# Where the triangular product of the routing gets its counts, and which PSUM banks some small products use

## The chip, the cores and the metric

The kernel runs on one core of one Trainium2 chip. The metric is the device time of one execution in microseconds (us). Engines are called PE or TensorE (matrix products), DVE or VectorE, ACT or ScalarE, POOL or GpSimd, and SP or SyncE (which here only issues transfers). A PSUM bank is 128 x 512 words of fp32 into which TensorE's products go and from which VectorE and ScalarE read them.

## What is computed

Three steps on 4 x 3584 = 14336 tokens of D = 192: a causal depthwise convolution of 7 taps, then a mixture of 8 experts (F = 1024), of which each token takes the best one, unless a skip gate lets the token pass, then a second mixture of 8 experts whose gate has a bias by modality. Cut to what matters:

```python
# convolution: 8 heads of 24 channels, softmax over the 7 taps of each head
out = np.einsum('hk,bskhg->bshg', w, x_unf)
# first mixture
do_compute = x @ w_skip > 0
xc = x[do_compute]
logits = xc @ w_gate
e_idx = np.argmax(logits, axis=1)
gate_w = softmax(logits)[e_idx]
y[e_idx == e] = gate_w * (np.maximum(xc @ w1[e], 0) @ w2[e])
out[do_compute] = xc + y
# second mixture: every token, no residual
logits = x @ w_gate2 + modality_bias[modality_id]
out[e_idx == e] = gate_w * (np.maximum(x @ w1[e], 0) @ w2[e])
```

The routing in between is done on the chip: every token of an expert gets a rank among that expert's tokens, and from the ranks come the lists by which the tokens are gathered in slots of 128.

## The kernel before, in words

**Stages.** The first stage runs over 128 tiles of 112 tokens, in NG = 8 groups of GT = 16 tiles, and each group has eight steps. A step (`run` of the first class, one value of `v`) does, for three groups that are at different points: six transposes of two tiles (`tr`, into bank 6 or 2), the rest of the preceding convolution product and the sum of the gate's halves on VectorE (`lows`, tiles `hl` and `L`), one head's convolution product (`conv`, banks 5, 0, 1 in turn), and the gate products of the tiles that were transposed two steps ago (`gm`, banks 7 and 4). Once per group `fin` makes gates and expert codes out of `L`, mostly on GpSimd, and SyncE stores the group's rows. After 64 + 12 steps the stage is over. When the lists of the first four groups (GA = 4) are there, the expert products begin (`Ffn`, slots of 128 tokens: gather, transposing transfer `xt`, products with `w1b` and `w2b`); the remaining steps of the first stage are done ahead of the first slots. In the last twelve steps the transposes use banks 6 and 5, and the gate products bank 7 and the words 352 to 487 of bank 5, since bank 2 belongs to the experts by then.

**Side work.** Beside these steps run generator tasks. Each `tick()` moves every task on by one; a task that did `yield n` sleeps for n ticks. A step has two ticks, at its `lows` and at its end. The routing of a group is such a task, `route_a`: it compares the codes with the eight expert numbers (`oha`), runs VectorE's scan over the 128 flags of each partition (`cuma`, 8 experts by 16 tiles, one running count), takes from the scan's last column of each expert the running totals `genda`, subtracts neighbours to get the counts `cnta`, multiplies these with a triangular matrix and one of ones (`tri`, `ones`: how many tokens lie on partitions below, and how many in all), copies the result from PSUM (`offa`), corrects the running counts on GpSimd, reduces them to `rank`, and turns ranks into slots and places (`sla`, `qa`), from which comparisons (`oa`, `ob`) and 16 products make the list. Two marks hand over between groups: a group starts when `res["A"]` has its number, and goes on to `rank` when `res["B"]` has it. The later routes (`ranks` and `invert`, called by `route`) do the same for more tokens with all of it on VectorE; they run while the experts run. Another set of tasks prepares the weights (scaled and split, tiles `w1b`, `w2b`, `ws`), with small products in banks 7 and 3.

**What sets the order.** Every engine works off its instructions as the program issues them: a wrapper (`InOrder`) ties each instruction to the one issued before it on its engine. So an instruction that waits holds up everything behind it, and where a task is after how many ticks decides what stands ahead and behind.

**Names.** Lines 126 to 139 hand out the banks: `misca` is 16 words of bank 3 for the product of `route_a`, `misc` 16 words of bank 3 for other small results and the product of `ranks`, `gram` the results of the preparation of weights (bank 7), `ptr1` and `pgt1` the transposes and gate products of the last twelve steps (lines 136 to 138), `acc` the lists (banks 3 and 5). Lines 401 to 414 hold the counts, the product and the correction, lines 440 and 441 the mark `res["A"]`, lines 481 to 504 `ranks`.

Nearly all instructions go through the wrapper and stand at line 70 in the profile, so they are told apart by the names of their tiles.

Of the kernel before, what the change touches and what calls it, by code (L numbers as in the profile page):

```python
# [7 lines left out]
F32 = mybir.dt.float32  # L8
# [4 lines left out]
ALU = mybir.AluOpType  # L13
# [14 lines left out]
GT = 16  # L28
# [86 lines left out]
class Moe:  # L115
    def __init__(self, tc, ctx):
# [4 lines left out]
        bk = [bp.tile([128, 512], F32, name=f"bank{i}") for i in range(8)]  # L121
        h = [b.bitcast(F16) for b in bk]
# [3 lines left out]
        self.acc = [bk[3], bk[5]]  # L126
        self.pt, self.pt2 = [h[4][:, 0:384]], [h[7][:, 512:896], h[3][:, 0:384]]
        self.pg2 = [bk[5][:, i:i + 64] for i in (0, 64, 128)]
        self.gram = [bk[7][:, 256:512], bk[7][:, 0:256]]
        self.misc = bk[3][:, 496:512]  # L130
        self.ph3 = bk[5]
        self.misca = bk[3][:, 240:256]
        self.pc0 = [bk[i][:TP, :384] for i in (5, 0, 1)]
        self.ptr0, self.ptr1 = ([h[i][:, :6 * TP] for i in p] for p in ((6, 2), (6, 5)))
        self.pgt0, self.pgt1 = ([bk[i][:, 0:136] for i in p] for p in ((7, 4), (7,)))
        self.pgt1.append(bk[5][:, 352:488])
        self.gramx = bk[3][:, 384:512]
# [236 lines left out]
    def route_a(self, g, code, pool, ob, res):  # L374
        nc = self.nc
# [5 lines left out]
        base = res["base"]  # L381
# [10 lines left out]
        oh = pool.tile([128, 8, GT], F32, name="oha")  # L392
        nc.vector.tensor_tensor(oh, cg.unsqueeze(1).to_broadcast([128, 8, GT]), self.c8.unsqueeze(2).to_broadcast([128, 8, GT]), ALU.is_equal)
        cum = pool.tile([128, 8, GT], F32, name="cuma")
# [3 lines left out]
        gend = pool.tile([128, 9], F32, name="genda")  # L398
        nc.gpsimd.memset(gend[:, 0:1], 0.0)
        nc.gpsimd.tensor_copy(gend[:, 1:9], cum[:, :, GT - 1])  # L400
        cnt = pool.tile([128, 8], F32, name="cnta")
        nc.gpsimd.tensor_tensor(cnt, gend[:, 1:9], gend[:, 0:8], ALU.subtract)
        pos = pool.tile([128, GT], F32, name="posa")
        nc.gpsimd.tensor_scalar(pos, cg, -float(SB * 128), float(8 * SB * 128), ALU.mult, ALU.add)
        yield 3
        pp = self.misca
        nc.tensor.matmul(pp[:, 0:8], self.tri, cnt, start=True, stop=True)
        nc.tensor.matmul(pp[:, 8:16], self.ones, cnt, start=True, stop=True)
        yield 2
        off = pool.tile([128, 16], F32, name="offa")  # L410
        nc.vector.tensor_copy(off, pp)
        nc.gpsimd.tensor_tensor(gend[:, 0:8], base, gend[:, 0:8], ALU.subtract)
        nc.gpsimd.tensor_tensor(gend[:, 0:8], gend[:, 0:8], off[:, 0:8], ALU.add)
        nc.gpsimd.tensor_tensor(base, base, off[:, 8:16], ALU.add)
        if g == GA - 1:
# [22 lines left out]
        nc.gpsimd.tensor_tensor(ok[:, 0], ok[:, 0], cg, ALU.mult)  # L438
        nc.gpsimd.tensor_tensor(cg, cg, ok[:, 0], ALU.subtract)
        yield 5  # L440
        res["A"] = g + 1
        for h in (2 * g, 2 * g + 1):
# [37 lines left out]

    def ranks(self, code, pool, lag, r, wait=4):
        nc = self.nc
# [9 lines left out]
        nc.vector.tensor_copy(gend[:, 1:9], cum[:, :, T - 1])  # L492
        cnt = pool.tile([128, 8], F32, name="cnt")
        nc.vector.tensor_tensor(cnt, gend[:, 1:9], gend[:, 0:8], ALU.subtract)
        yield wait
        pp = self.misc
        nc.tensor.matmul(pp[:, 0:8], self.tri, cnt, start=True, stop=True)
        nc.tensor.matmul(pp[:, 8:16], self.ones, cnt, start=True, stop=True)
        yield 2
        off = pool.tile([128, 17], F32, name="off")  # L500
        nc.vector.tensor_copy(off[:, 0:16], pp[:, 0:16])
        nc.vector.tensor_tensor(off[:, 0:8], off[:, 0:8], gend[:, 0:8], ALU.subtract)
        r.extend((oh, cum, off[:, 0:8], off[:, 8:16]))
        yield 1
# [869 lines left out]
```

## Time and profile before

| | before |
|---|---|
| median of 3 runs | 1078.73 us (1071.69 to 1083.71) |
| the profiled execution's own time | 1078.92 us, span 1077.1 us |
| granted clock of TensorE, mean | 0.941 |
| TensorE, matrix products busy | 967.9 us, 90% of the span |
| TensorE, weight loads (beside the products) | 802.2 us, 74% |
| VectorE busy | 688.7 us, 64% |
| ScalarE busy | 501.1 us, 47% |
| GpSimd busy | 628.5 us, 58% |
| moved by DMA | 165.35 MB |

Busy shares are averages over the whole span. The page cuts the span in 40 slices (27 us each): TensorE is busy for 6 to 8 tenths in the first 240 us and for 9 tenths or more in nearly all of the last two thirds. A matrix product counts as busy for as long as it takes, and takes twice as long where the clock is granted at 0.50; a clock of 1.00 is the full one. In a timeline a row may stand for several like instructions (x2, x16), and the brackets at its end say how long the engine stood idle before it and whose end it waited for.

### The profile page before, as it was taken

Reading aid. Unit: us, or ns where it says so; the run is one execution under the profiler, and the core shown is the slowest. Engines: PE = TensorE matmul, PEld = TensorE weight load, DVE = VectorE, ACT = ScalarE, POOL = GpSimd, SP = SyncE. Lnnn points to the kernel's source line nnn. Section 1 sums busy time; section 2 is a strip of 40 time slices with the busy share of each in tenths; the row PEclk is TensorE's granted clock in tenths of the full one; section 3 lists DMA queues with packets and bytes.
Section 4 is the critical chain, followed back from the end, with each engine's and each line's share of the span. In section 5 each row is a group of like instructions: output and inputs, shape, how many; then the busy total and the mean of one; then the engine's idle time right before and its main releaser. Section 6 shows DMA issues by size and latency. Waiting matters only on the chain. (4 is left out here: it accounts for less than half of the span.)

```text
span 1077.1 us, 27331 instructions
## 1 busy us (share of the span) xinstructions
PE 967.9 (90%) x10104; PEld 802.2 (74%) x10104; DVE 688.7 (64%) x1797; ACT 501.1 (47%) x919; POOL 628.5 (58%) x1113
## 2 busy tenths in 40 slices
PE   6688877799999879999899999999999899999993
PEld 4556666688888767888777877778787788888882
DVE  4376966769998889888446666667844344444441
ACT  3485743443665535455345555553233333333331
POOL 4044778776856836676447877774443555545531
PEclk9887876999999889999999999999999999999997
DMA  5666457665669737767973443333257333323340
GB/s 203 210 205 246 153 169 217 172 199 160 208 181 267 229 121 244 221 204 219 292 229 98 95 110 101 96 101 91 53 151 242 78 73 75 76 72 72 79 117 14
DMA packets 109135, 165.35 MB, mean 154 GB/s; under 512 B 80976, under 2 KB 86074, under 8 KB 103233
## 3 DMA queue, kind: packets, MB, share of 16 engines
q1 hardware_dynamic: 94368, 134.02, 39.9%
q0 software_dynamic: 13920, 28.87, 11.9%
q8 instruction: 81, 1.33, 0.5%
q10 hardware_dynamic: 704, 0.63, 0.2%
q14 instruction: 62, 0.50, 0.2%
HBM read 181.56 MB, written 58.42 MB: 223 GB/s over the span
## 5 line engine op out<-in xcount | busy, mean ns | idle before, releaser
L70 PEld LDWEIGHTS <-w1b 128*128 128x128 f16 x4840 | 374.4, 100 | 54.1 <-issue 18.5
L70 PE MATMUL bank<-xp,w1b 128*128 128x256 f16 x2200 | 263.7, 273 | 8.2 <-DMA w1b<-s1b 2.5
L70 PEld LDWEIGHTS <-ws 128*128 128x128 f16 (+2 forms) x2208 | 192.1, 100 | 67.0 <-DMA ws<-in_moe_w_dram 10.9
L70 PE MATMUL bank<-w2b,ws 128*128 128x384 f16 x1760 | 237.4, 286 | 0.2 <-issue 0.2
L70 DVE SCALAR_TENSOR_TENSOR ws<-bank,ws 128x512 f16<-128x512 f32 x220 | 151.4, 690 | 124.3 <-ACT ws L70 105.6
L70 POOL DMA_INDIRECT out_dram<-u,si x114 | 115.4, 1013 | 185.2 <-DVE u L70 58.7
L70 ACT ACTIVATE ws<-bank 128x512 f16<-128x512 f32 x220 | 130.6, 597 | 113.5 <-PE bank L70 102.7
L70 PE MATMUL bank<-xt,w1b 128*128 128x128 f16 x2640 | 170.1, 225 | 10.7 <-DVE hlo L70 6.9
L70 PE MATMUL bank<-w2b,hh 128*128 128x384 f16 x528 | 141.2, 334 | 1.0 <-DMA w2b<-s2a 1.0
L70 PE MATMUL bank<-w2b,hlo 128*128 128x192 f16 x528 | 131.8, 250 | 0.0
L70 ACT ACTIVATE u<-bank,c 128x192 f32<-128x192 f32 x114 | 48.1, 422 | 153.2 <-PE bank L70 118.1
L70 DVE SCALAR_TENSOR_TENSOR hlo<-bank,hh 128x512 f16<-128x512 f32 x132 | 90.3, 686 | 42.2 <-ACT hh L70 41.3
L70 DVE SCALAR_TENSOR_TENSOR u<-bank,c,u 128x192 f32<-128x192 f32 x114 | 47.6, 417 | 100.5 <-ACT u L70 84.5
L70 ACT ACTIVATE hh<-bank 128x512 f16<-128x512 f32 x132 | 76.7, 593 | 42.1 <-PE bank L70 40.7
L70 PEld LDWEIGHTS <-hh 128*128 128x128 f16 x528 | 53.4, 101 | 31.5 <-issue 3.3
L70 POOL DMA_INDIRECT gt<-rows,idx x64 | 64.0, 999 | 11.2 <-issue 9.3
L70 PE MATMUL bank<-xg,band 128*112 128x384 f32 x128 | 64.0, 593 | 0.3 <-DVE s L70 0.3
L70 ACT COPY xtb<-bank 128x672 f16<-128x672 f16 x64 | 46.5, 728 | 36.9 <-PE bank L70 36.5
L70 POOL DMA_INDIRECT gt<-rows,idxB x56 | 56.5, 1008 | 11.9 <-issue 7.0
L70 POOL TENSOR_TENSOR x2s<-x2s,xs 128x192 f32<-128x192 f32 x46 | 31.6, 688 | 53.7 <-DVE x2s L70 42.2
L70 PE MATMUL bank<-ob,oa 128*128 128x56 f16 (+2 forms) x446 | 49.7, 263 | 6.0 <-DVE ob L70 6.0
L70 PEld LDWEIGHTS <-hlo 128*128 128x128 f16 x528 | 52.9, 100 | 1.6 <-issue 1.5
(252 smaller groups left out, 1431.8 us busy)
## 6 DMA issues: line engine op xcount, KB each, us to landing
w1b<-s1b SPq DMA_DIRECT2D x59, 1024.0 KB
w2b<-s2b SPq DMA_DIRECT2D x59, 768.5 KB
ws<-in_moe_w_dram SPq DMA_DIRECT2D x16, 768.0 KB
rows<-hl SPq DMA_DIRECT2D x8, 1386.0 KB
xg<-in_x_dram SPq DMA_DIRECT2D x7, 1536.0 KB
ws<-in_moe_w_dram SPq DMA_DIRECT2D x16, 512.0 KB
ws<-in_moe_w_dram SPq DMA_DIRECT2D x32, 256.0 KB
s1a<-w1b SPq DMA_DIRECT2D x8, 1024.0 KB
```

The costliest lines, as they stand in the source:

```text
L70: r = f(*args, **kw)
```

## The change

In `route_a` the subtraction of neighbours moves behind the product. Instead of the counts the two products multiply the scan's last column of each expert (`cum[:, :, GT - 1]`, eight words 16 apart), and the differences are taken from the product's result. For that, `offa` has two rows of nine words with a zero ahead of each, and `cnta` is now the 2 x 8 differences, on GpSimd. The product is issued one tick later after the scan (4 for 3), the copy of its result one tick later after the product (3 for 2). `res["A"]` is set five ticks earlier, so the next group may start while this one still compares. In `ranks` the same is done on VectorE, and the wait ahead of the product goes from 4 to 6 ticks. Then banks: `misc` and the second `gram` go from banks 3 and 7 to bank 4, the gate products of the last twelve steps from bank 5 to bank 4; a list `pt` that nothing used goes.

```diff
-        self.pt, self.pt2 = [h[4][:, 0:384]], [h[7][:, 512:896], h[3][:, 0:384]]
+        self.pt2 = [h[7][:, 512:896], h[3][:, 0:384]]
         self.pg2 = [bk[5][:, i:i + 64] for i in (0, 64, 128)]
-        self.gram = [bk[7][:, 256:512], bk[7][:, 0:256]]
-        self.misc = bk[3][:, 496:512]
+        self.gram = [bk[7][:, 256:512], bk[4][:, 0:256]]
+        self.misc = bk[4][:, 496:512]
         self.ph3 = bk[5]
         self.misca = bk[3][:, 240:256]
         self.pc0 = [bk[i][:TP, :384] for i in (5, 0, 1)]
         self.ptr0, self.ptr1 = ([h[i][:, :6 * TP] for i in p] for p in ((6, 2), (6, 5)))
-        self.pgt0, self.pgt1 = ([bk[i][:, 0:136] for i in p] for p in ((7, 4), (7,)))
-        self.pgt1.append(bk[5][:, 352:488])
+        self.pgt0, self.pgt1 = ([bk[i][:, 0:136] for i in p] for p in ((7, 4), (7, 4)))
@@ route_a
         nc.gpsimd.tensor_copy(gend[:, 1:9], cum[:, :, GT - 1])
-        cnt = pool.tile([128, 8], F32, name="cnta")
-        nc.gpsimd.tensor_tensor(cnt, gend[:, 1:9], gend[:, 0:8], ALU.subtract)
+        off = pool.tile([128, 2, 9], F32, name="offa")
+        nc.gpsimd.memset(off[:, :, 0:1], 0.0)
         pos = pool.tile([128, GT], F32, name="posa")
         nc.gpsimd.tensor_scalar(pos, cg, -float(SB * 128), float(8 * SB * 128), ALU.mult, ALU.add)
+        yield 4
+        pp = self.misca
+        nc.tensor.matmul(pp[:, 0:8], self.tri, cum[:, :, GT - 1], start=True, stop=True)
+        nc.tensor.matmul(pp[:, 8:16], self.ones, cum[:, :, GT - 1], start=True, stop=True)
         yield 3
-        pp = self.misca
-        nc.tensor.matmul(pp[:, 0:8], self.tri, cnt, start=True, stop=True)
-        nc.tensor.matmul(pp[:, 8:16], self.ones, cnt, start=True, stop=True)
-        yield 2
-        off = pool.tile([128, 16], F32, name="offa")
-        nc.vector.tensor_copy(off, pp)
+        nc.vector.tensor_copy(off[:, :, 1:9], pp.rearrange("p (k c) -> p k c", k=2))
+        cnt = pool.tile([128, 2, 8], F32, name="cnta")
         nc.gpsimd.tensor_tensor(gend[:, 0:8], base, gend[:, 0:8], ALU.subtract)
-        nc.gpsimd.tensor_tensor(gend[:, 0:8], gend[:, 0:8], off[:, 0:8], ALU.add)
-        nc.gpsimd.tensor_tensor(base, base, off[:, 8:16], ALU.add)
+        nc.gpsimd.tensor_tensor(cnt, off[:, :, 1:9], off[:, :, 0:8], ALU.subtract)
+        nc.gpsimd.tensor_tensor(gend[:, 0:8], gend[:, 0:8], cnt[:, 0], ALU.add)
+        nc.gpsimd.tensor_tensor(base, base, cnt[:, 1], ALU.add)
...
         nc.gpsimd.tensor_tensor(cg, cg, ok[:, 0], ALU.subtract)
+        res["A"] = g + 1
         yield 5
-        res["A"] = g + 1
@@ ranks
-    def ranks(self, code, pool, lag, r, wait=4):
+    def ranks(self, code, pool, lag, r, wait=6):
...
-        cnt = pool.tile([128, 8], F32, name="cnt")
-        nc.vector.tensor_tensor(cnt, gend[:, 1:9], gend[:, 0:8], ALU.subtract)
+        po = pool.tile([128, 2, 9], F32, name="po")
+        nc.vector.memset(po[:, :, 0:1], 0.0)
         yield wait
         pp = self.misc
-        nc.tensor.matmul(pp[:, 0:8], self.tri, cnt, start=True, stop=True)
-        nc.tensor.matmul(pp[:, 8:16], self.ones, cnt, start=True, stop=True)
+        nc.tensor.matmul(pp[:, 0:8], self.tri, cum[:, :, T - 1], start=True, stop=True)
+        nc.tensor.matmul(pp[:, 8:16], self.ones, cum[:, :, T - 1], start=True, stop=True)
         yield 2
-        off = pool.tile([128, 17], F32, name="off")
-        nc.vector.tensor_copy(off[:, 0:16], pp[:, 0:16])
-        nc.vector.tensor_tensor(off[:, 0:8], off[:, 0:8], gend[:, 0:8], ALU.subtract)
-        r.extend((oh, cum, off[:, 0:8], off[:, 8:16]))
+        nc.vector.tensor_copy(po[:, :, 1:9], pp.rearrange("p (k c) -> p k c", k=2))
+        off = pool.tile([128, 2, 8], F32, name="off")
+        nc.vector.tensor_tensor(off, po[:, :, 1:9], po[:, :, 0:8], ALU.subtract)
+        nc.vector.tensor_tensor(off[:, 0], off[:, 0], gend[:, 0:8], ALU.subtract)
+        r.extend((oh, cum, off[:, 0], off[:, 1]))
```

Three places show where instructions stand now. First TensorE, at one group's triangular product. `bank_58` to `bank_65` are banks 0 to 7; `hl` with `ident` are transposes, `xg` with `band` the convolution. A minus is the order before, a plus that of the change.

```order
 L70 MATMUL bank_62<-g_203,xtb_105 128x34
 L70 MATMUL bank_61<-ssx,ones 128x1
-L70 MATMUL bank_61<-cnta,tri 128x8
-L70 MATMUL bank_61<-cnta,ones 128x8
 L70 LDWEIGHTS hl
 L70 MATMUL bank_60<-ident,hl 128x112
```

The two products stood ahead of a step's transposes; they are taken out here.

A few rows on in the same engine's order, behind the six transposes of that step and ahead of its convolution product:

```order
 L70 LDWEIGHTS hl
 L70 MATMUL bank_60<-ident,hl 128x112
+L70 MATMUL bank_61<-cuma,tri 128x8
+L70 MATMUL bank_61<-cuma,ones 128x8
 L70 MATMUL bank_63<-xg,band 112x384
 L70 LDWEIGHTS xtb_106
```

So the product moved by six transposes, and its operand is the scan's tile `cuma` now.

Second, VectorE in the same group, at the copy of the product's result (`offa`) and the reduction to `rank`; `w1b` is the preparation of weights, `gec` belongs to the gate.

```order
 L70 SCALAR_TENSOR_TENSOR w1b_77<-ws_314,wsc,w1b_77 128x512
 L70 TENSOR_SCALAR s<-s 128x1
+L70 COPY offa<-bank_61 128x2x8
 L70 SCALAR_TENSOR_TENSOR hl<-bank_58,s,hl 112x16x24
 L70 SCALAR_TENSOR_TENSOR gec<-gd,c_211 112x256
-L70 TENSOR_REDUCE rank<-cuma 128x16
 L70 SCALAR_TENSOR_TENSOR w1b_77<-ws_314,wsc,w1b_77 128x512
 L70 TENSOR_REDUCE L<-bank_65 112x68
 L70 SCALAR_TENSOR_TENSOR hl<-bank_59,s,hl 112x16x24
+L70 TENSOR_REDUCE rank<-cuma 128x16
```

`rank` went behind three more operations; the copy, not shown at its old place, went behind six.

Third, SyncE's queue where the first expert slots begin: `rows` are stores of a group's rows, `xt` the transposing transfers of a slot's gathered tokens, `ws` loads of weights. Before:

```order
L780 DMA rows<-hl 112x3168
L289 DMA ws_2253<-in_moe_w_dram 128x1024
L841 DMA_TRANSPOSE xt<-gt 128x3x128
L780 DMA rows<-hl 112x3168
L841 DMA_TRANSPOSE xt<-gt 128x3x128 x3
L295 DMA ws_2324<-in_moe_w_dram 64x1024 x2
```

And with the change:

```order
L288 DMA ws_2217<-in_moe_w_dram 128x1024
L781 DMA rows<-hl 112x3168 x2
L842 DMA_TRANSPOSE xt<-gt 128x3x128 x2
L294 DMA ws_2304<-in_moe_w_dram 64x1024 x2
L842 DMA_TRANSPOSE xt<-gt 128x3x128 x2
```

Both stores now stand ahead of the first transposes, and a load of weights stands among the first four of them.

## Rows read from the trace of the kernel before

**Rows 1.** The page's first line: the span of the profiled execution.

```profile
span 1077.1 us, 27331 instructions
```

**Rows 2.** Tile `cnta`: count, ns min/median/max; then who waited, us, times.

```profile
L70 POOL TENSOR_TENSOR cnta<-genda x8: 200/276/957, 70.7 to 200.4; 128x8 f32<-128x8 f32 x8
...
  PE bank L70: 14.3, 6
```

**Rows 3.** TensorE's timeline: start, us, engine, line, operation [idle before <-releaser].

```profile
71.47 0.59 PE L70 MATMUL bank<-cnta,tri 128*128 128x8 f32 x2 [3.10 <-POOL cnta L70]
...
87.70 0.59 PE L70 MATMUL bank<-cnta,tri 128*128 128x8 f32 x2 [2.36 <-POOL cnta L70]
...
125.33 0.59 PE L70 MATMUL bank<-cnta,tri 128*128 128x8 f32 x2 [2.10 <-POOL cnta L70]
...
143.40 0.39 PE L70 MATMUL bank<-cnta,tri 128*128 128x8 f32 x2 [2.91 <-POOL cnta L70]
...
177.74 0.39 PE L70 MATMUL bank<-cnta,tri 128*128 128x8 f32 x2 [2.40 <-POOL cnta L70]
...
200.66 0.39 PE L70 MATMUL bank<-cnta,tri 128*128 128x8 f32 x2 [1.41 <-POOL cnta L70]
```

**Rows 4.** Windows: length, busy PE PEld DVE ACT POOL (count), PEclk, DMA share, GB/s.

```profile
71.50:77.00 5.50, 5.50 (x38) 3.86 (x39) 2.78 (x11) 2.44 (x4) 2.17 (x7) 0.50 0.43 147
87.70:100.50 12.80, 12.80 (x97) 9.95 (x98) 4.78 (x19) 4.22 (x7) 5.05 (x19) 0.50 0.63 244
125.40:134.60 9.20, 9.20 (x66) 6.75 (x67) 7.57 (x25) 3.93 (x7) 5.88 (x15) 0.50 0.58 172
145.60:152.00 6.40, 6.40 (x55) 5.19 (x55) 2.81 (x9) 1.91 (x5) 2.82 (x12) 0.50 0.02 7
```

**Rows 5.** Windows again, same columns: the first stage's pieces, and the second route.

```profile
68.00:85.00 17.00, 13.90 (x150) 9.96 (x146) 13.03 (x39) 11.76 (x20) 11.06 (x38) 0.80 0.73 255
85.00:110.00 25.00, 21.09 (x200) 16.03 (x197) 16.56 (x54) 11.23 (x19) 10.24 (x35) 0.73 0.61 231
110.00:123.00 13.00, 12.76 (x156) 9.61 (x155) 12.08 (x38) 12.50 (x22) 10.13 (x28) 1.00 0.32 92
123.00:140.00 17.00, 14.90 (x128) 10.69 (x129) 14.91 (x45) 10.79 (x19) 11.74 (x32) 0.70 0.65 220
140.00:158.00 18.00, 12.39 (x146) 10.06 (x143) 12.62 (x39) 7.37 (x12) 12.71 (x34) 0.74 0.35 108
158.00:205.00 47.00, 37.06 (x412) 33.55 (x413) 29.98 (x83) 17.24 (x27) 35.66 (x91) 0.74 0.69 199
354.00:406.00 52.00, 40.34 (x459) 34.92 (x458) 46.11 (x114) 22.96 (x40) 30.98 (x44) 0.84 0.58 175
```

**Rows 6.** VectorE's timeline: three of the eight scans.

```profile
123.47 0.48 DVE L70 TENSOR_TENSOR_SCAN cuma<-oha 128x128 f32<-128x128 f32 x1
...
176.72 0.42 DVE L70 TENSOR_TENSOR_SCAN cuma<-oha 128x128 f32<-128x128 f32 x1
...
199.64 0.42 DVE L70 TENSOR_TENSOR_SCAN cuma<-oha 128x128 f32<-128x128 f32 x1
```

**Rows 7.** Timeline of SyncE's queue (SPq) and TensorE at the first expert slot.

```profile
155.88 1.31 SPq L841 DMA_TRANSPOSE xt<-gt  x1
157.28 0.51 SPq L780 DMA_DIRECT2D rows<-hl  x1
...
158.35 1.89 PE L70 MATMUL bank<-xt,w1b 128*128 128x128 f16 x16 [0.77 <-DMA xt<-gt]
```

**Rows 8.** TensorE's timeline, transposes of the last group.

```profile
172.15 0.72 PE L70 MATMUL bank<-ident,hl 112*128 112x112 f16 x6 [2.73 <-DVE L L70]
```

**Rows 9.** TensorE's timeline during the second route and behind it.

```profile
371.54 0.60 PE L70 MATMUL bank<-cnt,tri 128*128 128x8 f32 x2 [2.17 <-DVE cnt L70]
...
400.52 0.59 PE L70 MATMUL bank<-ssq,ones 128*128 128x2 f32 x2 [6.78 <-DVE ssq L70]
```

**Rows 10.** Tile `rank`: what VectorE, its engine, waited for, us, times.

```profile
  POOL cuma L70: 2.6, 2
```

## The prediction

> **What bounds the kernel now.** I read the page's span first: the profiled execution spans 1077.1 us [rows 1], its own time is 1078.92 us and the median of the three runs 1078.73, so the sum below, made against 1078.9, holds for the median too. The chain that ended last says nothing here (it holds the closing scatter), so I went to the waits of TensorE, which is busy for 90% of the span. The entry that the change touches is the largest between 60 and 240 us: the triangular product of `route_a` waits six times out of eight for GpSimd's `cnta`, 14.3 us together [rows 2]. The subtraction itself is short (median 0.276 us); it is late because it stands behind GpSimd's other work for the same tokens.
>
> Then I read each wait by itself [rows 3]: 3.10, 2.36, 2.10, 2.91, 2.40 and 1.41 us. Last, the same stage in windows. Behind each of the first four waits lies a stretch in which the granted clock is 0.50, the lower of its two levels: 5.5, 12.8, 9.2 and 6.4 us, 33.9 us in all, with TensorE busy throughout and VectorE busy for 17.9 us of it [rows 4]. So each wait is paid twice: as a wait, and as slow products behind it. The stage's own table [rows 5] shows what else could hold it. From 110 to 123 us, where there is no such wait, the clock is 1.00 and VectorE is busy for 12.08 of 13 us. That is the pace which this stage can reach, and VectorE sets it.
>
> **The change part by part.** *The product reads the scan's last column.* It is now released by the end of VectorE's scan. TensorE came to the third wait of [rows 3] at 125.33 − 2.10 = 123.23; the scan ended at 123.47 + 0.48 = 123.95, and the product now stands one tick (six transposes) later, so some 0.25 us may be left. I take 0.25 for each of the first four: 10.47 − 1.0 = 9.5 us. For the last two, TensorE arrives at 175.34 and 199.25 and the scan ends at 177.14 and 200.06, so 1.8 and 0.8 are left and 0.6 is saved twice [rows 3, 6].
>
> *What comes back, stage by stage.* A stage can't become shorter than its busiest other engine, nor than TensorE's own work at the full clock (its busy time less half of the slow stretch) [rows 4, 5]:
> 68 to 85 us (17): VectorE 13.03; TensorE 13.90 − 2.75 = 11.2. I take 14.0: 3.0 back.
> 85 to 110 (25): VectorE 16.56; TensorE 21.09 − 6.4 = 14.7. VectorE has 4.78 of its work in the 12.8 slow us and 11.8 in the other 12.2, so the two overlap badly: 18.5, 6.5 back.
> 110 to 123: nothing.
> 123 to 140 (17): VectorE 14.91, nearly full already; TensorE 14.90 − 4.6 = 10.3. I take 15.5: 1.5 back.
> 140 to 158 (18): VectorE 12.62; TensorE 12.39 − 3.2 = 9.2. The stage ends with a transpose that a queue issues at 155.88 ahead of the first expert product at 158.35 [rows 7]; no faster TensorE shortens these 2.5 us. What is ahead of them holds 2.91 of wait and 6.4 slow: 4.0 back.
> 158 to 205 (47): GpSimd 35.66. Two savings of 0.6, some of the slow clock (the mean is 0.74), and the banks: at 172.15 transposes wait 2.73 us for VectorE to read `L` [rows 8]. They write the first 336 words of bank 5, `L` is read from word 352 of it on, so here a bank is waited for as a whole. The change puts these gate products on bank 4, and this wait goes. GpSimd may ask for some of it back: 4.0.
> Sum: 3.0 + 6.5 + 1.5 + 4.0 + 4.0 = 19.0. From below it is bounded by nothing (the waits move), from above by the floors: 4.0 + 8.4 + 2.1 + 5.9 (2.66 of wait, 3.2 of clock) + about 5.5 = 25.9.
>
> *The ranks of the later routes* lose a small VectorE operation ahead of their product and get two more ticks; the second route's wait for it was 2.17 us [rows 9]. Around it VectorE is busy for 46.11 of 52 us [rows 5], so a wait taken away there mostly comes up again behind VectorE; the 6.78 us at 400.52 [rows 9] are already of that kind. Between 0 and the 5.9 us in which VectorE is idle I take 2.0. The additional memory fill and the wider subtraction lie on VectorE between much longer work; I price them at nothing, and with no cover at well under 1 us for each route.
>
> *What it adds.* GpSimd: a memory fill, and a 16-word subtraction for an 8-word one (0.276 [rows 2]), at most 0.3 us for each group, hidden but for the two groups after 158 us: 0.5. Ticks: one ahead of the product and one behind it. Two ticks are a step, and 13 us hold most of one group's eight steps [rows 5], so both cost at most 1.6 us; the first experts' lists are later by about that: 1.0. On SyncE's queue the first two transposes now stand behind a store of rows that one of them was ahead of. The transpose was issued at 155.88, the store at 157.28 [rows 7]; if the store is no earlier, the first expert product is 1.4 later, if its data come earlier, nothing. I take 1.4. Queued behind VectorE's copy of the product are the `hl` subtractions that free the convolution's banks, but the copy now comes three ticks after the product and finds it done. The product's operand has a stride of 16 words: 8 columns for each product, 0 to 0.3 us a group, I take 0.
>
> Net: 19.0 + 2.0 − 2.9 = 18.1, 1078.9 − 18.1 = 1060.8, about **1061 us**.
>
> **The rivals.** *All of the slow clock comes back.* Products at the full clock take half the time and the other engines follow. Half of 33.9 is 17.0; with 9.5 + 1.2 of waits, 2.7 of the bank, 2.0 and −2.9 that is 29.5, or 1049.4. For it: VectorE is busy in only half of the slow stretches. Against it are the floors: 68 to 85 would come to 17 − 2.85 − 2.75 = 11.4 us with 13.03 of VectorE in it, 123 to 140 to 10.6 with 14.91. With the floors kept it ends at 25.9 + 2.0 − 2.9 = 25.0, or 1053.9. The Trainium skill ("TensorE: Matmul & The Clock Gate", section Terms) has a rule of this kind: it prices time at half clock at half its length, which would make the time 1049.4. By that rule, stages one and four would be shorter than VectorE's work in the trace, so here it can only be an upper bound.
>
> *The clock stays down.* TensorE, no longer held up in one place, is held up in several by VectorE and falls to the lower clock all the same. Then only waits come back: 9.5 + 1.2 + 2.7, of which VectorE asks for about half again, 6.7 − 2.9 = 3.8: 1075.1. For it: VectorE's floor is 14.91 of 17 us in the fourth stage. Against it: from 110 to 123 VectorE is as full, and the clock is 1.00.
>
> *The wait moves to VectorE (slower).* GpSimd is as late as before, and `rank` on VectorE needs its `cuma`. TensorE's stop used to give GpSimd time: VectorE waited for it only twice, 2.6 us together [rows 10]. Now VectorE comes to `rank` earlier, and behind it in its queue stand `hl`, `L` and the gate, so TensorE, ScalarE and the next group wait too. With a wait of w in each of eight groups the price is 8w. It eats the gain at w = 18.1/8 = 2.3 us, and the kernel is slower by over 1% (10.8 us) from 28.9/8 = 3.6 us. Against it: between product and `rank` there are now six ticks instead of five, between scan and `rank` ten instead of eight.
>
> **How the numbers follow.** The forecast (1054 to 1068) gets 0.50, all of the clock 0.13, the clock that stays down (1068 to 1079) 0.28, the wait on VectorE 0.09, most of it beyond 1%. A change of 1% is about what a measurement of this kernel can tell from none; 1068.1 and 1089.7 are the lines. Faster: 0.50 + 0.13 = 0.63; same: 0.28 and a little of the last, 0.30; slower 0.07. The range goes from 1047, the floors' 1053.9 less about half the 12 us by which the three runs differ, to 1078, which takes in nearly all of the clock that stays down.
>
> **What would show it.** In the profile after: no entry of TensorE waiting for GpSimd's counts, the product released by the scan or by nothing; a granted clock of 1.00 in the pieces that answer to 71 to 77 and 88 to 100; VectorE busy for over 85% from 68 to 140; no wait of transposes for `L` once the experts run. Wrong would be: as many microseconds at 0.50 as before (the clock stays down); idle time of VectorE ahead of `rank` well over 2.6 us (the wait moved); or a gain before 205 us that is lost again between 205 and 410, where the weights and the second route's ranks stand.

## The result: slower by 1.3%, and where the profile after shows it

| | before | after |
|---|---|---|
| median | 1078.14 us (4 runs, 1071.69 to 1083.71) | 1091.92 us (4 runs, 1088.63 to 1094.33) |
| ratio | | 1.0132, 95% interval 1.0090 to 1.0174 |
| profiled execution's span | 1077.1 us | 1090.0 us |
| granted clock, mean | 0.941 | 0.949 |

Measured again beside its variants the ratio was 1.0105 (1.0069 to 1.0141). The ratios here and below leave out executions over 1.5% above the fastest of the same kernel, which matters for one kernel alone (`after_r2w4`: three of its ten go, and with all ten the medians would give 1.0089 for 1.0050). The forecast was 1061 us, 1.7% faster. The page of the kernel after says little: the engines do the same work in a longer span, so TensorE stands idle longer.

```profile
span 1090.0 us, 27340 instructions
...
PE 966.1 (89%) x10104; PEld 800.7 (73%) x10104; DVE 689.4 (63%) x1800; ACT 500.4 (46%) x919; POOL 628.8 (58%) x1121
```

The waits of TensorE in the kernel after (what it waited for: us in all, times, longest) have no entry for GpSimd's counts any more, the 14.3 us of [rows 2]. The scan that took their place costs 5.4, nearly all of it in one wait behind the first expert slot (4.67 us at 171 us). But the waits for the transposed tokens of the first expert slots, for VectorE's list-making (`ob`) and for the preparation of weights (`ssq`) have grown. Before:

```profile
PE bank L70 <- DVE ssq L70: 7.4, 2, 6.8
...
PE bank L70 <- DVE ob L70: 6.0, 6, 2.0
...
PE bank L70 <- DMA xt<-gt: 3.8, 2, 3.0
```

And after:

```profile
PE bank L70 <- DMA xt<-gt: 14.1, 2, 8.3
PE bank L70 <- DVE ob L70: 13.1, 11, 2.8
PE bank L70 <- DVE ssq L70: 12.1, 7, 4.7
...
PE bank L70 <- DVE cuma L70: 5.4, 2, 4.7
```

To see where, I cut both executions at the same pieces of work, by the starts of three of ScalarE's operations in its timeline: the 49th copy of transposed tokens (`xtb`), the 1st, 25th and 81st hidden result of the experts (`hh`), the 47th, 67th and 113th output (`u`). Windows of the kernel before (columns as in [rows 4]); the first is the stage of the change from 68 us on:

```profile
68.00:135.10 67.10, 57.75 (x566) 43.06 (x563) 52.00 (x157) 41.59 (x69) 39.89 (x120) 0.77 0.59 207
...
135.10:160.70 25.60, 19.64 (x225) 15.65 (x225) 17.22 (x53) 12.05 (x20) 18.02 (x52) 0.77 0.47 154
160.70:255.70 95.00, 80.35 (x943) 70.20 (x942) 68.56 (x161) 37.36 (x59) 71.56 (x149) 0.83 0.72 208
255.70:424.40 168.70, 148.82 (x1907) 130.13 (x1904) 150.13 (x369) 95.19 (x167) 109.89 (x156) 0.94 0.66 193
424.40:776.00 351.60, 334.90 (x3540) 281.48 (x3539) 240.63 (x669) 173.84 (x352) 228.81 (x401) 0.99 0.53 151
776.00:868.40 92.40, 87.83 (x798) 72.11 (x796) 41.70 (x96) 32.03 (x61) 44.88 (x61) 1.00 0.53 145
868.40:1056.40 188.00, 188.00 (x1673) 154.48 (x1672) 84.64 (x182) 73.02 (x137) 93.29 (x130) 1.00 0.31 79
```

The same pieces after:

```profile
68.00:125.60 57.60, 49.21 (x565) 37.28 (x562) 49.49 (x153) 40.70 (x68) 39.91 (x116) 0.96 0.66 234
...
125.60:156.00 30.40, 19.42 (x237) 15.60 (x237) 16.99 (x59) 14.66 (x23) 24.69 (x67) 0.72 0.55 175
156.00:248.50 92.50, 75.58 (x881) 66.38 (x880) 65.35 (x156) 34.29 (x57) 65.50 (x147) 0.86 0.65 196
248.50:429.60 181.10, 157.64 (x1968) 136.54 (x1965) 149.58 (x370) 95.40 (x168) 108.95 (x156) 0.93 0.66 187
429.60:781.80 352.20, 333.12 (x3522) 280.25 (x3521) 246.09 (x669) 174.22 (x352) 229.97 (x401) 0.99 0.52 149
781.80:882.50 100.70, 92.38 (x800) 74.97 (x799) 43.37 (x99) 32.08 (x61) 43.71 (x60) 0.95 0.49 132
882.50:1071.00 188.50, 188.50 (x1678) 154.91 (x1676) 84.69 (x182) 72.97 (x137) 93.96 (x132) 1.00 0.31 79
```

The stage of the change gained 9.5 us, with the clock at 0.96 for 0.77. Then three pieces lost: 4.8 us at the first expert slot, 12.4 from 255 to 424 us, 8.3 from 776 to 868. The first lies just behind the changed code; the other two lie where `route_a` has long ended. A part of the second is work that moved: the piece ahead of it holds 62 of TensorE's products fewer than before (881 for 943) and is 2.5 us shorter, and the second holds 61 more (1968 for 1907). The two pieces together lose 9.9 us.

### The profile page after: what moved, and what is told of

It reads as the page before. It is cut to its first block, busy times and chain, and to the rows that moved or that the text cites. A ratio compares the mean times of both kernels' runs of the same rounds, so it can differ in the third digit from the quotient of the medians.

```text
span 1090.0 us, 27340 instructions
## 1 busy us (share of the span) xinstructions
PE 966.1 (89%) x10104; PEld 800.7 (73%) x10104; DVE 689.4 (63%) x1800; ACT 500.4 (46%) x919; POOL 628.8 (58%) x1121
## 5 line engine op out<-in xcount | busy, mean ns | idle before, releaser
L70 PEld LDWEIGHTS <-w1b 128*128 128x128 f16 x4840 | 375.8, 101 | 63.5 <-issue 20.8
L70 PE MATMUL bank<-xt,w1b 128*128 128x128 f16 x2640 | 172.8, 226 | 21.4 <-DMA xt<-gt 14.1
L70 PE MATMUL bank<-ob,oa 128*128 128x56 f16 (+2 forms) x446 | 49.8, 263 | 18.5 <-DVE ob L70 13.1
L70 POOL TENSOR_TENSOR x2s<-x2s,xs 128x192 f32<-128x192 f32 x46 | 35.2, 765 | 50.6 <-DVE x2s L70 37.2
L70 PEld LDWEIGHTS <-oa 128*128 128x128 f16 x446 | 45.1, 151 | 22.2 <-issue 17.8
L70 PE MATMUL bank<-xg,band 128*112 128x384 f32 x128 | 58.8, 548 | 2.1 <-DVE hl L70 1.4
```

Of the source, the lines that this page charges most:

```text
L70: r = f(*args, **kw)
```

## The experiments

Each kernel was also profiled and cut at the same marks. Lengths of the four pieces that move, in us, and the measured ratio to runs of the kernel before beside it ("block" is explained at the drain, below):

| kernel | to 49th copy | first slot | 25th to 81st hidden | drain | ratio (95% interval) |
|---|---|---|---|---|---|
| before | 135.1, again 132.0 | 25.6, 27.3 | 168.7, 170.7 | 92.4, 97.2 | 1 |
| `banks` | 129.4 | 26.2 | 168.3 | 89.3 | 0.9967 (0.9927 to 1.0006) |
| `ranks` | 128.7 | 27.2 | 170.5 | 97.4 (block) | 1.0062 (1.0022 to 1.0103) |
| `src` | 124.0 | 24.1 | 170.7 | 92.8 | 0.9894 (0.9832 to 0.9957) |
| `best` | 122.4 | 24.1 | 170.6 | 95.2 | 0.9896 (0.9859 to 0.9933) |
| `after_ot` | 123.0 | 24.1 | 170.6 | 98.2 (block) | 0.9969 (0.9939 to 1.0000) |
| `routea` | 125.3 | 30.5 | 169.5 | 92.4 | 1.0017 (0.9976 to 1.0059) |
| `after_wait4` | 126.0, again 125.9 | 31.2, 30.6 | 169.2, 167.9 | 91.4, 94.9 | 0.9961 (0.9922 to 0.9999), 0.9978 (0.9947 to 1.0008) |
| `wait4_store` | 121.3 | 26.3 | 170.8 | 97.4 | 0.9948 (0.9918 to 0.9978) |
| the change | 125.6, again 123.5 | 30.4, 30.5 | **181.1, 180.5** | 100.7, 95.1 (block) | 1.0132 (1.0090 to 1.0174), 1.0105 (1.0069 to 1.0141) |
| `after_store` | 124.4 | 26.2 | **178.3** | 98.3 (block) | 1.0088 (1.0048 to 1.0128) |
| `after_r2w4` | 125.2 | 31.4 | **180.5** | 92.9 | 1.0050 (1.0008 to 1.0092) |
| `after_r1w4` | 124.7 | 31.1 | 169.3 | 96.9 (block) | 1.0050 (1.0012 to 1.0087) |
| `after_wait8` | 124.5 | 30.8 | 168.5 | 100.3 (two blocks) | 1.0034 (0.9999 to 1.0069) |
| `after_skip1` | 123.8 | 31.2 | 171.1 | 95.9 (block) | 1.0038 (0.9994 to 1.0081) |
| `after_two` | 119.2 | 30.6 | 171.0 | 93.9 | 0.9973 (0.9937 to 1.0008) |
| `after_three` | 125.5 | 26.2 | 171.8 | 88.8 | 1.0003 (0.9957 to 1.0049) |

The other pieces vary too (90.0 to 99.9 us, 345.8 to 356.8 us, 188.0 or 188.5, and 18.1 to 24.4 us behind the last mark), and two executions of one kernel lie up to 7 us apart in them; what moves them stays open.

### The parts alone

`banks`, lines 126 to 138 only:

```diff
-        self.gram = [bk[7][:, 256:512], bk[7][:, 0:256]]
-        self.misc = bk[3][:, 496:512]
+        self.gram = [bk[7][:, 256:512], bk[4][:, 0:256]]
+        self.misc = bk[4][:, 496:512]
...
-        ... ((7, 4), (7,)))
-        self.pgt1.append(bk[5][:, 352:488])
+        ... ((7, 4), (7, 4)))
```

> The kernel before with the banks of the change alone (misc, second gram and the last gate products on bank 4). Theory Q (the loss comes from the extra ticks, which put the store of rows ahead of the first transposing transfers and shift the side work): this part is harmless and takes away the 2.73 us wait of transposes for L, 1072 to 1079 us. Theory B (small products that share bank 4 wait for each other): most of the loss is here, 1086 to 1094 us.

0.9967: no measurable difference, and no loss. The wait for `L` of [rows 8] is there in `ranks` (2.31 us) and `src` (2.66) with the old banks, and gone in `banks` and `best`. (`routea`, also with the old banks, doesn't have it either: the new ticks move it away by themselves.) But nothing was gained by that, for the time is waited for a little later, at the product of the next group. In `src`, with the old banks, and then in `best`, with the new ones:

```profile
159.51 0.72 PE L70 MATMUL bank<-ident,hl 112*128 112x112 f16 x6 [2.66 <-DVE L L70]
164.55 0.60 PE L70 MATMUL bank<-cuma,tri 128*128 128x8 f32 x2 [1.86 <-DVE cuma L70]
```

```profile
163.59 0.59 PE L70 MATMUL bank<-cuma,tri 128*128 128x8 f32 x2 [4.75 <-DVE cuma L70]
```

The two waits of `src` make 4.52 us, the one of `best` 4.75: the wait only moved. Theory B falls.

`routea` is the whole diff of `route_a` on the kernel before; `src` the same without the ticks and without the earlier mark:

```diff
-        yield 4
+        yield 3
         pp = self.misca
...
-        yield 3
+        yield 2
         nc.vector.tensor_copy(off[:, :, 1:9], pp.rearrange("p (k c) -> p k c", k=2))
...
-        res["A"] = g + 1
         yield 5
+        res["A"] = g + 1
```

> The kernel before with the whole part in route_a (product from the scan, ticks 4 and 3, earlier mark A), banks and ranks of before. Theory Q: the first expert product waits some 8 us for its transposes again, and the later stages lose as in the change, 1085 to 1094 us. Theory R (the two more ticks in ranks put the later routes' VectorE work in bad places and cost what is lost behind 214 us): the early gain stays, 1066 to 1076 us.

> The kernel before with the product reading the scan's column and the differences taken behind it, but with the ticks 3 and 2 and the mark A of before; banks and ranks of before. The first transposing transfer is ahead of the second store on SyncE's queue, as before. Theory Q: the gain of the first stage stays, first expert slot 8 to 12 us earlier than before, 1066 to 1073 us. Theory L (whatever the first stage gains is asked back by VectorE and the transfers of weights later): slot earlier too, but 1075 to 1090 us.

`src` took 1062.54 us beside 1071.87 for the kernel before, so reading the scan is worth 1%, and the later stages don't ask that back: theory L falls. `routea`, 1074.68, gave it back (1.0017, not to be told from the kernel before), but it was not as slow as the change: theory Q is only a part. `ranks` is the diff of `ranks` alone:

> The kernel before with the part in ranks alone (product from the scan, wait of 6 ticks for 4). Theory Q: no measurable difference, 1074 to 1082 us. Theory R: the pieces from 214 to 530 us are longer by about 12 us, as in the change, 1086 to 1094 us.

1078.72 us, ratio 1.0062: theory R is not nothing either. But its loss is in the last piece (97.4), not from 214 to 530 us where I had put it. The three parts make +0.5% together, the change +1.05%. That hints at parts which make each other worse, but with four tenths of a per cent of uncertainty in each part it doesn't show it.

### The first expert slot

`after_again` is the change, beside three variants. `after_store` holds one store back:

```diff
         self.codes = g + 1
         yield 2
+        if g == 5:
+            while len(m.xq) < 2:        # the transposes issued so far
+                yield 1
+            with m.tc.issue_after(m.xq[1].ins):
+                self.store(g, meta)
+            return
         self.store(g, meta)
```

SyncE is not among the four engines whose order the wrapper ties. In all ten profiles with `route_a`'s new ticks and no store held back, the second store stands ahead of the first transposes; in all seven with the old ticks it stands behind the first of them.

> The change itself once more, beside its variants on one chip. From the parts measured alone (route_a with its ticks +2.8 us, ranks +6.8, banks -2.8 against 1071.9) a plain sum gives 1078.7 us; if it is 1084 or more again, the parts make each other worse.

> The change, with one difference: the second of the two stores that stand ahead of the first transposing transfers on SyncE's queue stands behind the first two of them; no other engine's order differs. Theory S (the store's 1386 KB go through the same queue ahead of the transposes, so the first expert product waits 8.3 us): the wait falls to 3 us or less and the slow clock behind it shrinks, time 6 to 10 us below that of the change. Theory W (the transposes wait for the gathered tokens anyway): wait and time unchanged within 2 us.

`after_again` took 1081.42 us, between the plain sum and the 1084, so the total alone left it open. In the change, SyncE's queue in the timeline:

```profile
131.56 15.70 SPq L781 DMA_DIRECT2D rows<-hl  x2
147.37 5.20 SPq L842 DMA_TRANSPOSE xt<-gt  x2
```

GpSimd began to issue the first gather at 144.05, and TensorE waits 8.27 us for the transposed tokens:

```profile
144.05 1.21 POOL L70 DMA_INDIRECT gt<-rows,idxa  x1 [0.19 <-issue]
```

```profile
153.66 2.31 PE L70 MATMUL bank<-xt,w1b 128*128 128x128 f16 x20 [8.27 <-DMA xt<-gt]
```

In `after_store`, SyncE's queue and TensorE:

```profile
145.75 2.60 SPq L849 DMA_TRANSPOSE xt<-gt  x2
148.44 0.53 SPq L788 DMA_DIRECT2D rows<-hl  x1
```

```profile
148.23 2.31 PE L70 MATMUL bank<-xt,w1b 128*128 128x128 f16 x20 [4.12 <-DMA xt<-gt]
```

From issue to product the first transposes take 6.3 us behind the store (153.66 − 147.37) and 2.5 without it (148.23 − 145.75). So it is in every profile: 6.2 to 7.3 us in the ten with the store ahead, 2.5 in the ten others. The packets in the trace of the change have the same order: those of the store run from 147.78 to 152.76 us, those of the transposes begin at 151.69. The other part of the wait is that nothing is left to do: in the program's order 61 of the 64 steps' transposes now stand ahead of the first slot, where it was 60, so one step fewer is left to cover the gather. Neither theory came true as it stood: the store is about half of the wait (8.27 to 4.12 us, not to 3), and in time `after_store` brought nothing that can be told (1.0088 for 1.0105), with the wait of 4 0.3% (below).

`after_ot` and `after_wait4` take the new ticks away on one side each, `yield 3` and `yield 2` in `route_a`, or `wait=4` in `ranks`:

> The change with the ticks 3 and 2 of before in route_a (the mark A early, banks and ranks as in the change). Theory S: the first transpose is ahead of the second store again, and 8 to 12 us come back. If ticks and ranks are all of the loss, the sum of parts gives about 1062.5 + 6.8 - 2.8 = 1066.5 us; theory L (later stages ask the gain back): 1075 us or more.

> The change with a wait of 4 ticks in ranks as before, its product still read from the scan. Theory R (the two more ticks move the later routes): 5 to 8 us below the change. If it is the reading from the scan that costs: no difference, within 2 us.

1066.91 and 1064.79 us beside 1081.42: 14.5 and 16.6 us come back, where alone the ticks of `route_a` cost 12.1 (`routea` less `src`) and `ranks` 6.8. So `ranks` costs more in company than alone. That is the piece from the 25th to the 81st hidden result: long only in kernels with both. My theory R had nothing on why.

### The slots from 250 to 430 us

A slot of the experts has four ticks. So has a round of the list-making (`oa`, `ob`, its eight products). So one round falls in every slot, and whatever is ahead of the rounds decides once for all of them at which point of a slot the products stand. With a wait of 4 they stand behind the first half of a slot's products, with 6 at its very end, ahead of the next slot. That made three experiments:

```diff
-    def ranks(self, code, pool, lag, r, wait=6):      # after_wait8
+    def ranks(self, code, pool, lag, r, wait=8):
...
-        for w in self.ranks(code, pool, 1, r):        # after_r1w4 ("1"), after_r2w4 ("2")
+        for w in self.ranks(code, pool, 1, r, wait=4 if tag == "1" else 6):
```

> The change with a wait of 8 ticks in ranks for 6. A slot of the experts has four ticks and a round of the list-making in the later routes (oa, ob, product) has four too, so the wait sets at which point of every slot the list's product stands. Theory P (this point is what costs): with 8 it is the point of wait 4 again, and the eight to thirteen slots that took 79 us in the change (and 72 with wait 4) take 71 to 73; the last route, which is drained at a fixed slot, is later still, with two blocks of products left for the drain instead of one, so the stretch that takes 92.3 us before (from 776 to 868 us) takes 97 or more. Total 1070 to 1076 us. Theory M (the later the routes, the worse): 81 us or more in the slots, total 1084 us or more.

> The change with a wait of 4 ticks in the first of the later routes alone. Theory P: the slots that took 79 us take 71 to 73, the drain's stretch stays at 95 to 100, total 1071 to 1076 us. If the lateness of the route and not its point in a slot costs: between, 75 us or more in these slots, total 1077 us or more.

With 8 the piece is 168.5 us, with 4 in the first route alone 169.3 (in time 1.0034 and 1.0050 for 1.0105): a later route isn't slower, one at the wrong point is (theory M falls). But `after_ot` and `ranks` have their products at that point too and take 170.6 and 170.5. What they don't have is the weight preparation two ticks of its own earlier, which `route_a`'s ticks bring about. `after_skip1` holds the preparation back by one tick, once:

```diff
             if i < n2:
...
-                tkw.tick()
+                if i >= 11:
+                    skip[0] += 1
+                if i < 11 or skip[0] > 1:
+                    tkw.tick()
```

> The change with one tick of the weight preparation withheld once, at the twelfth slot, and nothing else: from there the preparation stands beside the list-making as in the kernel that has the change with the old ticks in route_a (which had the list's product at the same point of a slot and lost nothing). Theory C (it is the coincidence of the list-making with the preparation of weights on VectorE that costs, and neither alone): the slots that take 180 to 181 us in the change and 170.6 there (hidden result 24 to 80 on ScalarE) take 169 to 173, total 8 to 11 us below the change, a ratio to before of 0.998 to 1.003. Theory P alone (the point of the list's product in a slot is enough): no difference, ratio 1.010.

171.1 us for 180.5: the coincidence it is. In time it brought 0.7% (1.0038 for 1.0105, with intervals that overlap a little), somewhat less than expected. The order of TensorE's products says the same of all twenty profiles. In the four with a long piece an `ssq` product comes straight behind a round of `ob` products three times, and a fourth time with only products of the weight preparation between; in `ranks`, `after_ot`, `after_skip1`, `after_two` and `after_three` once; in the others never. TensorE at one of these places, first `after_again`:

```profile
294.35 0.61 PE L70 MATMUL bank<-ob,oa 128*128 128x6 f16 x8 [0.78 <-DVE ob L70]
296.75 0.59 PE L70 MATMUL bank<-ssq,ones 128*128 128x2 f32 x2 [1.79 <-DVE ssq L70]
297.20 2.29 PE L70 MATMUL bank<-xt,w1b 128*128 128x128 f16 x20
```

And `after_skip1`:

```profile
293.60 0.60 PE L70 MATMUL bank<-ob,oa 128*128 128x6 f16 x8 [0.78 <-DVE ob L70]
294.06 1.28 PE L70 MATMUL bank<-xt,w1b 128*128 128x128 f16 x20
...
296.88 0.38 PE L70 MATMUL bank<-ssq,ones 128*128 128x2 f32 x2 [0.53 <-DVE ssq L70]
```

In the change two small products that wait for VectorE stand one behind the other ahead of the slot's twenty: 0.78 and 1.79 us of idle time, and then the twenty take 2.29 us for 1.28. The granted clock during the twenty, in `after_again` and in `after_skip1`:

```profile
297.20:299.49 2.29, 2.29 (x23) 2.29 (x24) 2.22 (x10) 0.42 (x1) 0.62 (x2) 0.50 1.22 219
```

```profile
294.06:295.34 1.28, 1.28 (x26) 1.28 (x25) 1.28 (x3) 0.95 (x3) 1.11 (x3) 1.00 1.08 440
```

One tick apart, the slot's work stands between them, and the second waits only 0.53 us. The whole piece, `after_again` and then `after_skip1`:

```profile
246.70:427.20 180.50, 157.24 (x1967) 135.86 (x1965) 149.19 (x370) 95.61 (x168) 109.10 (x156) 0.93 0.65 187
```

```profile
247.50:418.60 171.10, 150.27 (x1955) 130.57 (x1952) 151.44 (x370) 95.71 (x168) 111.38 (x156) 0.96 0.66 194
```

Of the 9.4 us, TensorE's idle time is 2.4 (23.3 and 20.8) and its busy time 7.0, with 12 products more of nearly 2000 and a mean clock of 0.93 for 0.96: most is paid as slower products, not as waits.

### The drain

The last route is not waited for but drained: at a fixed slot all that is left of it is issued at once. With two ticks more, one whole round (`oa`, `ob`, eight products) is left for that place, the "block" of the table: the piece holds 36 list products for 28, and with the wait of 8, two blocks, 44. `after_r2w4` gives the last route alone its 4 ticks:

> The change with a wait of 4 ticks in the last route alone (6 in the two others). Its list-making is then drained as before, with no block of products in the drain. Theory D (the drain is what costs in the stretch that takes 92.3 us before): 91 to 93 us for 95 to 100, total 5 to 8 us below the change, 1073 to 1077 us. If the drain is harmless: no difference, 1080 to 1083 us.

Its drain piece was 92.9 us, its ratio 1.0050 for 1.0105, with intervals that overlap, so in time the drain's price is not shown. (The profiled execution, 1092.26 us, is the longest of its ten.) Over all kernels the piece takes 95.1 to 100.7 us with the block (8 profiles, mean 97.9) and 88.8 to 97.4 without it (12, mean 93.2): 4.6 us, with ranges that overlap, and one profile each way proves little (the kernel before had 97.2 the second time). What all eight have and none of the twelve is a wait for `ob` of 1.7 to 1.9 us. In the change TensorE waits first for the block, and then for weights and tokens:

```profile
792.21 0.81 PE L70 MATMUL bank<-ob,oa 128*128 128x58 f16 x6 [1.69 <-DVE ob L70]
824.80 0.32 PE L70 MATMUL bank<-w2b,hh 128*128 128x384 f16 x1 [2.09 <-DMA w2b<-s2b]
```

The gathers of the list's tokens start when the list is there, and GpSimd waits 3.34 us for it in the change, 1.28 before:

```profile
795.08 0.96 POOL L70 DMA_INDIRECT gt<-rows,idx  x1 [3.34 <-DVE idx L70]
```

```profile
787.22 0.96 POOL L70 DMA_INDIRECT gt<-rows,idx  x1 [1.28 <-DVE idx L70]
```

### Do the places account for all of it?

`best` has all that reads the scan, the new banks and the earlier mark, and every old wait:

> The change with every wait of before: ticks 3 and 2 in route_a, 4 in ranks; product from the scan in both, earlier mark A, new banks. By the parts (product from the scan 1062.5, banks -2.8): 1058 to 1062 us. Theory L (the later stages ask the early gain back): 1066 us or more.

0.9896: it beats both kernels, and equals `src`. (Its 1068.24 us lie in the range of theory L, but the kernel before took 1077.28 beside it: times are to be compared only on one chip, and the ratio is what the parts gave.) `after_two` is the change with the withheld tick and 4 ticks in the last route, `after_three` has the store held back as well; `wait4_store` holds it back with 4 ticks everywhere in `ranks`:

> The change with the withheld tick of the preparation and 4 ticks in the last route, the store as in the change. Both this and the one with 4 ticks everywhere take away the coincidence and the block in the drain, by different means: the same time within 3 us if these two places are the whole cost of the wait of 6. If the withheld tick costs something of its own: 5 us or more above it.

> The change with a wait of 4 ticks in ranks, once more, as the comparison for the two beside it: a ratio to before of 0.992 to 1.000, as in the first run (0.996).

> The change with 4 ticks in ranks and with the second store behind the first two transposes. If the 3 to 4 us that the profile shows at the first expert slot are real in time: 3 to 5 us below the one beside it. If something later asks them back (with the 6 ticks the timed runs showed 0 of them): within 2 us of it.

> The change with its ticks, and three remedies at once: the store behind the first two transposes, the withheld tick of the preparation, and 4 ticks in the last route. If the three places are all of the loss: 4 + 10 + 6 = 20 us below the change, a ratio to before of 0.989 to 0.996, near the kernel with all old waits (0.990). If something else of the change costs too: 0.998 or more.

`after_two` (0.9973) equals the kernel with 4 ticks everywhere (0.9978, and 0.9961 before), so as far as intervals of four tenths of a per cent tell, the coincidence and the drain are the whole cost of the wait of 6. The store held back brings 0.3% there, 2.5 us, between the two expected cases and with intervals that overlap.

> The kernel before once more, for a second profile: how far its first stage (135.1 us to the 49th copy of transposed tokens in the first profile, 129 in two kernels with the same first stage) varies from one execution to another. If the first profile was a late one, 127 to 131 us.

132.0 us: the first stage varies by some 6 us between executions of the same code (128.7 to 135.1 with four profiles).

From the means of the table's columns: the scan read by the product −7.3 us in the first stage (131.3 to 124.0) and −2.5 at the first slot with the old ticks (26.6 to 24.1); `route_a`'s ticks +6.7 (30.8); the store held back −4.6 (26.2); the coincidence +10.1 (180.1 for 170.0); the block +4.6. Added up for each kernel, against the measured change (1% is 10.7 us):

| kernel | sum | measured | kernel | sum | measured |
|---|---|---|---|---|---|
| the change | +1.1% | +1.3%, +1.1% | `after_r1w4` | +0.1% | +0.5% |
| `src` | −0.9% | −1.1% | `after_wait8` | +0.1% | +0.3% |
| `best` | −0.9% | −1.0% | `after_skip1` | +0.1% | +0.4% |
| `after_ot` | −0.5% | −0.3% | `after_two` | −0.3% | −0.3% |
| `after_wait4` | −0.3% | −0.4%, −0.2% | `wait4_store` | −0.7% | −0.5% |
| `after_store` | +0.7% | +0.9% | `after_three` | −0.7% | 0.0% |
| `after_r2w4` | +0.7% | +0.5% | `routea` | −0.3% | +0.2% |
| `ranks` | +0.4% | +0.6% | `banks` | 0 | −0.3% |

The sums come from the profiles alone, and most hit the timed ratio within its interval. `routea` misses it narrowly (−0.3% for an interval from −0.24%). `after_three` misses it clearly: 0.7% more than its places say, though its profile shows all three mended. Why its timed runs are longer than that (1062.5 to 1077.5 us) stays open, as does the store's worth in time.

## Why the prediction was wrong, step by step

**The reading of the kernel before was right.** The product is released by the scan, the 14.3 us of waits are gone (what was to be left of the last two, 1.8 and 0.8 us, measured 1.86 and 0.87 in `src`), and the clock is up: pieces of the stage after,

```profile
68.00:81.00 13.00, 11.13 (x141) 8.11 (x138) 11.48 (x37) 10.69 (x19) 9.48 (x31) 1.00 0.84 298
81.00:95.00 14.00, 13.18 (x145) 10.49 (x144) 11.04 (x37) 6.70 (x13) 10.41 (x37) 0.88 0.86 344
95.00:113.00 18.00, 16.19 (x190) 11.99 (x189) 15.18 (x51) 15.74 (x26) 10.55 (x31) 1.00 0.34 109
113.00:125.60 12.60, 8.70 (x92) 6.68 (x91) 11.79 (x30) 7.57 (x13) 9.47 (x21) 0.95 0.72 226
```

have 1.00, 0.88, 1.00 and 0.95, and VectorE is busy for 49.49 of 57.6 us, 86%, as "over 85%" had it. TensorE is as busy (49.21), so that VectorE alone now sets the pace is not shown.

**"Stage by stage", 19.0 us, was about twice too large.** The first three terms (3.0 + 6.5 + 1.5 = 11) measured 7.3, with some 6 us between executions; the fourth (4.0) measured 2.5; of the last (4.0, up to 205 us) nothing is to be seen in the piece from the 1st to the 25th hidden result (92.9 us on the mean with the counts, 93.4 in `src`, `best` and `after_ot`), although the wait for `L` did go: it came up again at the next group's product (4.67 us in the change and 4.75 in `best`, for 1.86 in `src`). In the first stage, too, the waits I had counted as gain mostly moved: from 68 us to the 49th copy TensorE is idle for 9.4 us before (67.10 − 57.75) and for 8.4 after. What came back is the clock: busy 57.75 and 49.21 us for the same products, 8.5 less. By the mean clocks (0.77 in 67.1 us, 0.96 in 57.6) the time at 0.50 fell from 30.9 us to 4.6. The Trainium skill ("TensorE: Matmul & The Clock Gate", section Terms) prices slow time at half its length. By that rule, an estimate, 13.1 us would have come back, so here too it is an upper bound. (The twenty products above took 1.8 times as long at 0.50 as at 1.00, 2.29 us for 1.28.)

**"Ticks: 1.0" and "I take 1.4" for the store** measured 6.7 together at the first slot. I had priced a tick as a length of time, and the store as an issue slot. The tick pushed a whole step of the first stage ahead of the slot, and the store is a transfer of 1386 KB with the transposes behind it in the queue: of the wait of 8.27 us the store is about 4. The prediction said "if the store is no earlier": it asked when the store was issued, not how long what is behind waits for it.

**"The ranks of the later routes: 2.0" had the wrong sign**, and this is the step that decided. I took the operation that goes as the gain and the two ticks as cover. With the old wait that gain is nothing that can be told (`best`, which has it, equals `src`, which does not). The two ticks cost 4.6 us at the drain, and with `route_a`'s ticks 10.1 at the slots. So this term is off by 16.7 us, the stages by 9.2 and the ticks with the store by 4.3: 30.2 in all, which makes +12 of the forecast's −18, where 11 (second measurement) to 14 us (first) were measured. Nothing in the views of the kernel before shows that directly. But the 6.78 us for `ssq` in [rows 9] stood there as a wait for VectorE in just this stretch, where VectorE is busy for 46.11 of 52 us [rows 5]; it should have been read as "here a shift costs", not as "here a gain is lost". The order of TensorE's instructions has the new place of the `ob` products in every slot; the prediction weighed only `route_a`'s places.

**The rivals.** The slower one was "the wait moves to VectorE" at `rank`. It did grow, to 3.7 us in six times, against 2.6 in two [rows 10]; far from the 2.3 us in each group from which it would decide:

```profile
  POOL cuma L70: 3.7, 6
```

No rival had the mechanism that came. The sign by which I would know, "a gain before 205 us that is lost again between 205 and 410, where the weights and the second route's ranks stand", came true in part: the slots lie there, the first slot's loss ahead of it and the drain's far behind. But it was a sentence without a chance or a price. With 0.07 for slower I held for nearly excluded what an untimed shift of two generators against each other can do.

## What to carry to other kernels

When side work is placed by counting ticks, a changed wait is not a delay but a phase: compare its period with that of the main loop, and list for every later loop what now stands next to what, above all small products that wait for another engine one behind the other. Make the change of data and the change of timing apart: here the data path alone gave 1.0% and the longer waits that came with it took 2%. And look for what is drained or issued at a fixed place, since a little lateness turns there into a whole block.

## What the runs showed of the hardware that was not expected

Most of a short wait's price is not the wait: in the coincidence 2.4 us of additional idle time came with 7.0 us of longer products, and in the first stage nearly all of the gain was the clock (0.77 to 0.96) at almost the same idle time. There, 9.4 us of idle time with waits of up to 3.10 us went with the lower clock, and 8.4 us in twice as many waits, none over 1.8, with the higher one; whether it is the length of the waits that decides was not tested by itself. And a transposing transfer that is issued right behind a store of 1386 KB on one queue had its product start 6.3 us after issue, for 2.5 with the store behind it. Last, taking away a bank's wait of 2.7 us gave nothing, since the next product, 5 us later, waited that much longer.
